# Twelve attention units whose values come out as queries by features, with the softmax sum as a 65th column

## The chip, the cores and the metric

One core of a Trainium2 chip runs the whole program in one launch. The metric is the device time of one execution in microseconds (us); lower is better. Engines are named as in the profile: PE (TensorE, matrix products; PEld its weight loads), DVE (VectorE), ACT (ScalarE), POOL (GpSimd), SP (the queue that issues DMAs).

## The reference, cut to what matters

Three stages follow each other: attention over a window of 128 keys with a distance bias, an expert layer with a squared ReLU, and a mixture of eight experts whose gates are balanced by 8 rounds of normalisation. The change touches the first.

```
B, H, S, D = 4, 8, 576, 64
scores = q @ k.T / sqrt(D)
bias   = slopes[h] * -(|i - j|)              # slopes 2^-(8 (h+1) / H)
scores = where(0 <= i - j < 128, scores + bias, -1e9)
attn   = exp(scores - max(scores));  attn /= sum(attn) + 1e-9
x      = (attn @ v), heads side by side      # 2304 tokens x 512 features
x      = square(relu(x @ w_in)) @ w_out      # first expert layer
out    = sum over 8 experts of gate * relu(x @ w1) @ w2
```

## The kernel before

The attention is cut into 32 units of one batch, two heads (a pair `hp`) and one of two parts: the first 384 queries (three tiles `i` = 0, 1, 2 of 128 queries) or the rest (`rest`: tile 3 of 128 queries and the tail, tile 4, in which 64 queries of both heads share the 128 partitions). The first 12 units (`WHOLE_UNITS`, L56) are worked in a form in which one PSUM bank holds the scores of both heads; these are the four first-part units and the four `rest` units of batch 0, and the four first-part units of batch 1.

Three steps make up a unit, and `plan` (L393) writes down their order. "q" (`attention_qk`, L205) transposes keys and queries. "s" (`attention_scores`, L268) multiplies a tile's queries with two blocks of keys (L289 adds the bias by a product with the identity, L295 the scores), takes the row minimum on DVE (L299), the exponential on ACT with its sum `z` (L314), adds 1e-9 and inverts on DVE (L318, L319) and multiplies the weights `s` by it (L321). "t" transposes the weights block by block (`attention_weights`, L324; PE L345, ACT copy L346 into `p`) and forms the values (`attention_values`, L368, through `block`, L348, PE L354). There the stationary operand is `v` with its 64 features, up to 256 queries move, and the two heads fill the two halves of the output's partitions, so that `xo` is features by queries. `xo` is allocated at tile 1 (in `rest` units at the tail) and complete after the last tile; `put_x` (L359) splits it into the two parts `xh` (ACT, L114) and `xl` (DVE, L115), which the first expert layer reads.

Units 0 to 3 come first, two by two, in an order with two tiles of lead; then chunk 0 of the first expert layer (384 tokens, 16 steps `f`) starts with product `h` (L119 to L121, called from `gemm1`, L123). In each step `part` (L670) advances the attention by a share of the steps of units 4 to 11. In the same steps DVE and ACT convert the 64-bit expert weights (`narrow`, L452), two tiles a step. Units 12 to 31 run beside the later chunks in another form and stay as they are.

PSUM has eight banks of 512 columns here: `ps_acc` (4), `ps_mm` (1) and `ps_at` (3). Units 0 to 3 may use all of them (`at_ps`, L165, by a running count), later units only the three of `ps_at`: for transposed keys and queries (`tp`), scores (`sc`), transposed weights (`pt`) and `xo`.

Up to L738 a planner orders the instructions: it goes by the order in which they were written and by its own idea of when each can run, and fixes each engine's queue. PE's queue and the others run in that order.

Of the kernel before, what the change touches and what calls it, by code (L numbers as in the profile page):

```python
# [8 lines left out]
F32 = mybir.dt.float32  # L9
# [14 lines left out]
def raw(ap):  # L24

    return ap.bitcast(F32)
# [3 lines left out]
def attention_moe_moe2(  # L30
# [12 lines left out]
    nc = tc.nc  # L43
    P = 128
    B, H, S, D = q.shape
# [5 lines left out]
    FULL = S // P  # L51
    TAIL = S - FULL * P
    CH = 512

    EARLY = 3 * P
# [24 lines left out]
    def chunk(c):  # L80
        return starts[c], widths[c]

    xh, xl = [], []
# [11 lines left out]
    ident = const.tile([P, P], F32, name="ident")  # L95
# [17 lines left out]
    def split_ps(ps, hi, lo):  # L113
        nc.scalar.activation(hi, ps, AF.Copy)  # L114
        nc.vector.tensor_sub(lo, ps, raw(hi))  # L115
# [19 lines left out]
    SETS = 2  # L135
# [4 lines left out]
    ap = att.enter_context(tc.tile_pool(name="ap", bufs=1, side="right"))  # L140
# [22 lines left out]
    xo_early = [(ps_mm, "mm"), (ps_acc, "acc")]  # L163

    def at_ps(name, t, many=early):  # L165
        pool, tag = many[psn[0] % len(many)] if t["alone"] else (ps_at, "at")
        psn[0] += 1
        return pool.tile([P, 512], F32, name=name, tag=tag)

    qtail, qwhole = [], []  # L170
    for i in range(SETS):

        qtail.append(ap.tile([P, 2, TAIL], F32, name=f"qtail{i}"))
        qwhole.append(ap.tile([P, 7 * P], F32, name=f"qwhole{i}"))
        nc.gpsimd.memset(qwhole[i], 0.0)

    def tails_ready():

        for i in range(SETS):
            nc.gpsimd.memset(qtail[i], 0.0)  # L180
        for hp in range(NPAIR):
            for j in range(2):
                nc.scalar.copy(
                    tbias[j * TAIL : (j + 1) * TAIL, hp, :], raw(bias[0:TAIL, 2 * hp + j, : P + TAIL])
                )
# [69 lines left out]
    def attention_v(n, t):  # L255

        rest = t["rest"]
        vw = t["v"] = ap.tile([P, 3, 2, D], F32, name="v", tag="v", bufs=2)
        b, hp, _ = units[n]
        for j in range(2):  # L260
            src = v[b, 2 * hp + j]
            if rest:
                nc.sync.dma_start(vw[:, :2, j], src[2 * P : FULL * P].rearrange("(t p) d -> p t d", p=P))
                nc.sync.dma_start(vw[:TAIL, 2, j], src[FULL * P :])
            else:
                nc.sync.dma_start(vw[:, :, j], src[:EARLY].rearrange("(t p) d -> p t d", p=P))

    def attention_scores(hp, t, i):  # L268

        tail = i == FULL  # L270

        kb0, qb0 = (2, 3) if t["rest"] else (0, 0)
        nk = min(S, (i + 1) * P) - max(0, i - 1) * P
        k0 = (max(0, i - 1) - kb0) * P
        c0 = 2 * P - nk if i == 0 else 0
        heads = 1 if tail else 2

        if t["whole"]:
            bank = at_ps("sc", t)
            scs = [bank[:, j * nk : (j + 1) * nk] for j in range(heads)]  # L280
        else:
            scs = [at_ps("sc", t) for j in range(heads)]
        s = ap.tile([P, 2, 2 * P], F32, name="s", tag="s", bufs=3)
        m = ap.tile([P, 2], F32, name="m", tag="m", bufs=3)
        z = ap.tile([P, 2], F32, name="z", tag="z", bufs=3)
        if t["whole"]:
            bj = tbias[:, hp, :nk] if tail else bias[:, 2 * hp : 2 * hp + 2, c0 : c0 + nk]
            sv = bank[:, : heads * nk].rearrange("p (j c) -> p j c", j=heads)
            nc.tensor.matmul(  # L289
                bank[:, :nk] if tail else sv, lhsT=ident_r, rhs=bj, start=True, stop=False,  # L290
                skip_group_check=True,
            )
            for j, sc in enumerate(scs):
                q0 = 6 * P if tail else (2 * (i - qb0) + j) * P
                nc.tensor.matmul(  # L295
                    sc, lhsT=t["qw"][:, q0 : q0 + P], rhs=t["kf"][:, k0 : k0 + nk], start=False, stop=j == heads - 1,
                    skip_group_check=True,
                )
            nc.vector.tensor_reduce(out=m[:, :heads], in_=sv, op=ALU.min, axis=AX.X)  # L299
        else:  # L300
            for j, sc in enumerate(scs):
                r = slice(0, P) if tail else slice(j * D, (j + 1) * D)
                lhs = t["qt"].rearrange("p j c -> p (j c)") if tail else t["qf"][r, (i - qb0) * P : (i - qb0 + 1) * P]
                nc.tensor.matmul(sc[:, :nk], lhsT=lhs, rhs=t["kf"][r, k0 : k0 + nk], start=True, stop=True)
        for j, sc in enumerate(scs if not t["whole"] else ()):
            bj = raw(tbias[:, hp, :nk] if tail else bias[:, 2 * hp + j, c0 : c0 + nk])
            nc.vector.tensor_tensor_reduce(
                out=s[:, j, :nk], in0=sc[:, :nk], in1=bj, scale=1.0, scalar=3.0e38,
                op0=ALU.add, op1=ALU.min, accum_out=m[:, j : j + 1],
            )  # L310
        if tail:
            nc.gpsimd.memset(s[:, 0, nk:], 0.0)
        for j in range(heads):
            nc.scalar.activation(  # L314
                s[:, j, :nk], scs[j][:, :nk] if t["whole"] else s[:, j, :nk], AF.Exp, bias=m[:, j : j + 1], scale=-1.0,
                accum_out=z[:, j : j + 1],
            )
        nc.vector.tensor_scalar_add(z[:, :heads], z[:, :heads], 1e-9)  # L318
        nc.vector.reciprocal(z[:, :heads], z[:, :heads])  # L319
        for j in range(heads):  # L320
            nc.vector.tensor_scalar_mul(s[:, j, :nk], s[:, j, :nk], z[:, j : j + 1])  # L321
        t[i] = s

    def attention_weights(t, i):  # L324

        s, tail, blocks = t[i], i == FULL, 2 if i else 1

        if not t["p"]:
            t["p"] = ap.tile([P, 2, 6 * P], F32, name="p", tag="p", bufs=2)
        kb0 = 2 if t["rest"] else 0  # L330
        at = max(0, 2 * (i - kb0) - 1) * P
        pt = at_ps("pt", t)
        if tail:
            for kb in range(2):
                nc.tensor.transpose(pt[:, kb * P : (kb + 1) * P], s[:, 0, kb * P : (kb + 1) * P], ident)
            for kb, rows in ((0, P), (1, TAIL)):
                c = at + kb * P
                nc.scalar.copy(
                    t["p"][:rows, :, c : c + TAIL], pt[:rows, kb * P : (kb + 1) * P].rearrange("p (j c) -> p j c", j=2)
                )  # L340
            return
        pv = pt[:, : 2 * blocks * P].rearrange("p (j c) -> p j c", j=2)
        for j in range(2):
            for kb in range(blocks):
                nc.tensor.transpose(pv[:, j, kb * P : (kb + 1) * P], s[:, j, kb * P : (kb + 1) * P], ident)  # L345
        nc.scalar.copy(t["p"][:, :, at : at + blocks * P], pv)  # L346

    def block(t, kb, dst, a, w, first, last):  # L348

# [6 lines left out]
                start=first, stop=last, skip_group_check=True,  # L356
            )

    def put_x(ps, hp, t0, n):  # L359
        o = 0  # L360
        while o < n:
            c = max(c for c in range(NCH) if starts[c] <= t0 + o)
            at = t0 + o - starts[c]
            w = min(n - o, widths[c] - at)
            split_ps(ps[:, o : o + w], xh[c][:, hp, at : at + w], xl[c][:, hp, at : at + w])
            o += w

    def attention_values(b, hp, t, i):  # L368

        if i == 1:  # L370
            xo = t["xo"] = at_ps("xo", t, [xo_early[hp % 2]])
            block(t, 0, xo[:, : 2 * P], 0, 2 * P, True, False)
        if i == 2:
            xo = t["xo"]
            block(t, 1, xo[:, P : 3 * P], 0, 2 * P, False, False)
            block(t, 2, xo[:, 2 * P : 3 * P], 0, P, False, True)
            put_x(xo, hp, b * S, EARLY)
        if i == FULL:
            xo = at_ps("xo", t)
            block(t, 3, xo[:, : P + TAIL], 0, P + TAIL, True, False)  # L380
            block(t, 2, xo[:, :P], P, P, False, False)
            block(t, 4, xo[:, P : P + TAIL], 0, TAIL, False, True)
            put_x(xo, hp, b * S + EARLY, P + TAIL)
# [301 lines left out]
    for c in range(NCH):  # L685
        c0, n = chunk(c)
# [15 lines left out]
        for f in range(NF1):  # L702
            now[:] = c, f
            a, bw = ahead.pop(0)
# [4 lines left out]
            hp, tag = (ps_mm, "mm") if c < NCH - 1 else (ps_at, "at")  # L709
# [3 lines left out]
            r = rp.tile([P, CH], F32, name="r", tag="r", bufs=2)  # L713
# [10 lines left out]
            if len(pending) > LAG:  # L724
                t = pending.pop(0)
# [558 lines left out]
```

## Time and profile before

| | us |
|---|---|
| median of 3 runs | 2118.92 |
| lowest, highest | 2118.63, 2123.6 |
| profiled execution, whole | 2118.78 |
| its span in the trace | 2117.0 |

All views are of the one profiled execution, and times in them are microseconds from the start of its span. "Busy" adds up the durations of instructions; on PE matrix products overlap, so the distance from one start to the next tells more of what an instruction costs than its duration. A wait is idle time of an engine just before an instruction, put down to what ended it.

### The profile page before, as it was taken

How to read it: one execution, taken by the hardware profiler on the slowest of the kernel's cores; microseconds unless marked ns; L12 is line 12 of the kernel's file. 1: busy time of each engine (PE TensorE's matmuls, PEld its weight loads, DVE VectorE, ACT ScalarE, POOL GpSimd, SP SyncE). 2: the span in 40 equal slices, each digit the busy share in tenths (PEclk: the TensorE clock that was granted, in tenths of full speed). 3: DMA queues.
4: the chain of work that ended last, by engine and by line, in shares of the span. 5: the costliest groups of instructions: out<-in, count | busy, mean ns of one | idle time of the engine just before them, and what ended most of it. 6: DMA issues, size and time to landing. Idle time of an engine off the chain costs nothing.

```text
span 2117.0 us, 31449 instructions
## 1 busy us (share of the span) xinstructions
PE 2052.1 (97%) x11056; PEld 1859.8 (88%) x11056; DVE 1430.3 (68%) x2396; ACT 958.4 (45%) x1902; POOL 1032.7 (49%) x665
## 2 busy tenths in 40 slices
PE   6999999999998899999999999999999999999998
PEld 4877777777897787899998999999999999999998
DVE  7886444432327888877778676777768676777766
ACT  7775444433334444444444534444445534444343
POOL 1112212122437777888887444455456444455452
PEclk9999999999999999999999999999999999999999
DMA  7686756555667877887888977777887878777773
GB/s 213 227 253 209 230 154 178 158 181 171 210 202 265 294 264 282 307 319 288 309 313 296 319 264 260 256 253 254 266 264 260 271 264 259 256 250 258 264 262 125
DMA packets 281981, 525.43 MB, mean 248 GB/s; under 512 B 85840, under 2 KB 130016, under 8 KB 277728
## 3 DMA queue, kind: packets, MB, share of 16 engines
q1 hardware_dynamic: 281824, 523.42, 73.5%
q8 instruction: 89, 1.46, 0.3%
q14 instruction: 68, 0.56, 0.1%
HBM read 379.60 MB, written 143.73 MB: 247 GB/s over the span
## 4 chain that ended last, share of the span: by engine, by line
PE 59%; DVE 9%; ACT 2%; issue 2%; DMA 1%; POOL 1%; SPq 0%; ACTq 0%; DVEq 0%; POOLq 0%
PE y L120 9%; PE y L121 9%; PE y L119 9%; PE g L119 9%; PE g L121 9%; PE g L120 9%; DVE rl L954 1%; DVE o L922 1%; ACT rh L953 1%; DMA d_w<-w2a 1%; DVE o L920 1%; DVE s L644 1%; DVE s L642 1%; PE acc L120 1%; PE acc L121 1%
## 5 line engine op out<-in xcount | busy, mean ns | idle before, releaser
L1104 POOL TENSOR_TENSOR rb<-R,rb 128x768 fp32r<-128x768 f32 x95 | 212.7, 2239 | 334.6 <-ACT rb L1099 306.2
L1135 DVE TENSOR_TENSOR a<-y,a 128x384 f32<-128x384 f32 x434 | 239.7, 553 | 180.1 <-PE y L121 178.2
L1104 POOL TENSOR_TENSOR rt<-R,rt 128x768 fp32r<-128x768 f32 x125 | 238.9, 1924 | 146.1 <-issue 61.7
L111 POOL TENSOR_TENSOR gl<-r,gh 128x512 fp32r<-128x512 f32 (+1 forms) x80 | 97.1, 1214 | 397.7 <-ACT gh L110 379.1
L111 POOL TENSOR_TENSOR w2a<-r,w2a 128x1024 fp32r<-128x1024 f32 x64 | 155.4, 2430 | 67.5 <-ACT w2a L110 67.5
L1099 ACT ACTIVATE rt<-R 128x768 fp32r<-128x768 f32 x128 | 107.7, 841 | 148.7 <-DVE R L1086 90.2
L119 PE MATMUL g<-xt,w1o 128*128 128x384 f32 x512 | 172.7, 337 | 0.8 <-ACT u L827 0.6
L121 PE MATMUL g<-xt,w1o 128*128 128x384 f32 x512 | 172.4, 337 | 0.0
L119 PE MATMUL y<-rt,w2o 128*128 128x384 f32 x512 | 172.2, 336 | 0.1
L120 PE MATMUL g<-xt,w1o 128*128 128x384 f32 x512 | 172.2, 336 | 0.0
L121 PE MATMUL y<-rt,w2o 128*128 128x384 f32 x512 | 172.2, 336 | 0.0
L120 PE MATMUL y<-rt,w2o 128*128 128x384 f32 x512 | 172.0, 336 | 0.0
L120 PE MATMUL y<-w2a,rh 128*128 128x512 f32 x384 | 151.0, 393 | 0.2 <-POOL w2a L111 0.2
L119 PE MATMUL y<-w2a,rh 128*128 128x512 f32 x384 | 151.1, 393 | 0.0
L121 PE MATMUL y<-w2a,rl 128*128 128x512 f32 x384 | 150.1, 391 | 0.0
L1081 DVE TENSOR_TENSOR R<-R,pb 128x768 f32<-128x768 f32 x128 | 137.8, 1078 | 5.2 <-ACT R L1194 2.4
L716 DVE SCALAR_TENSOR_TENSOR r<-h,r 128x512 f32<-128x512 f32 (+1 forms) x80 | 50.9, 636 | 128.8 <-ACT r L714 128.7
L119 PE MATMUL y<-rb,w2o 128*128 128x384 f32 x384 | 129.8, 338 | 2.8 <-DVE a L1135 2.1
L120 PE MATMUL y<-rb,w2o 128*128 128x384 f32 x384 | 130.0, 339 | 2.4 <-POOL rb L1104 2.4
L121 PE MATMUL y<-rb,w2o 128*128 128x384 f32 x384 | 129.8, 338 | 0.0
L121 PE MATMUL g<-xb,w1o 128*128 128x384 f32 x384 | 129.1, 336 | 0.0
L119 PE MATMUL g<-xb,w1o 128*128 128x384 f32 x384 | 129.0, 336 | 0.0
(232 smaller groups left out, 5892.1 us busy)
## 6 DMA issues: line engine op xcount, KB each, us to landing
w1o<-d_w SPq DMA_DIRECT2D x448, 256.0 KB, 3.1
w2o<-d_w SPq DMA_DIRECT2D x224, 512.0 KB, 4.0
d_w<-w1a SPq DMA_DIRECT2D x32, 1792.0 KB, 11.6
d_w<-w2a SPq DMA_DIRECT2D x32, 1536.0 KB, 7.9
a<-d_in SPq DMA_DIRECT2D x64, 512.0 KB, 3.6
b<-d_out SPq DMA_DIRECT2D x64, 512.0 KB, 3.6
r<-in_moe_w_dram SPq DMA_DIRECT2D x64, 512.0 KB, 4.3
u<-in_moe_w_in_dram SPq DMA_DIRECT2D x16, 512.0 KB, 5.1
```

Of the source, the lines that this page charges most:

```text
L111: (eng or nc.gpsimd).tensor_sub(lo, src, raw(hi))
L119: nc.tensor.matmul(ps, lhsT=lh, rhs=rh, start=first, stop=False, **kw)
L120: nc.tensor.matmul(ps, lhsT=lh, rhs=rl, start=False, stop=False, **kw)
L121: nc.tensor.matmul(ps, lhsT=ll, rhs=rh, start=False, stop=last, **kw)
L642: nc.vector.tensor_sub(w1s[n][:, 2], w1s[n][:, 1], a11)
L644: nc.vector.tensor_sub(w1s[n][:, 0], a12, w1s[n][:, 2])
L716: nc.vector.scalar_tensor_tensor(g[:, :n], ph[:, :n], 0.0, r[:, :n], op0=ALU.max, op1=ALU.mult)
L920: nc.vector.tensor_add(acc[e][:, i], y, acc[e][:, i])
L1081: nc.vector.tensor_mul(r, r, pb[:, None, :].to_broadcast([P, 2, HALF]))
L1099: nc.scalar.activation(x[:, 0], R[m, f, h], AF.Copy)
L1104: eng.tensor_sub(x[:, 1], R[m, f, h], raw(x[:, 0]))
L1135: nc.vector.tensor_add(acc[dst][:, dt], ps[:, :HALF], acc[dst][:, dt])
```

## The change

For the 12 whole units the weights `s` are transposed as they come out of the exponential, without the multiplication by the inverse sum. In the value product the operands change places: a block of transposed weights `p` is stationary (128 keys by 128 queries) and `v` moves, with a 65th column of ones, so that a bank `xq` (128 queries by 65 columns per tile and head) holds the values and the sum of the weights. `vones` are two fixed buffers for `v` whose 65th column is set once. After a unit's last tile one addition, one reciprocal and one multiplication with a broadcast normalise all its tiles, and two or three transposes bring the result to features by queries in a bank `xt`, from which `put_x` goes on; in a `rest` unit it is called three times instead of once. `xq` is allocated at the unit's first tile. The exponential no longer writes its sum.

```diff
+        vones.append(ap.tile([P, 3, 2, D + 1], F32, name=f"vones{i}"))
+        nc.gpsimd.memset(vones[i][:, :, :, D:], 1.0)
...
     def attention_v(n, t):
-        vw = t["v"] = ap.tile([P, 3, 2, D], F32, name="v", tag="v", bufs=2)
+        if t["whole"]:
+            t["v"] = vones[n % SETS]
+            vw = t["v"][:, :, :, :D]
+        else:
+            vw = t["v"] = ap.tile([P, 3, 2, D], F32, name="v", tag="v", bufs=2)
...
     def attention_scores(hp, t, i):
-                accum_out=z[:, j : j + 1],
+                accum_out=None if t["whole"] else z[:, j : j + 1],
             )
+        t[i] = s
+        if t["whole"]:
+            return
         nc.vector.tensor_scalar_add(z[:, :heads], z[:, :heads], 1e-9)
...
     def attention_weights(t, i):
-        if not t["p"]:
+        if t["whole"]:
+            t["p"] = ap.tile([P, 4 * P], F32, name="pw", tag="pw", bufs=3)
+        elif not t["p"]:
...
-        nc.scalar.copy(t["p"][:, :, at : at + blocks * P], pv)
+        if t["whole"]:
+            nc.scalar.copy(t["p"][:, : 2 * blocks * P], pt[:, : 2 * blocks * P])
+        else:
+            nc.scalar.copy(t["p"][:, :, at : at + blocks * P], pv)
...
+    def values_by_query(b, hp, t, i):
+        rest, tail, blocks, W = t["rest"], i == FULL, 2 if i else 1, D + 1
+        u, slots = i - (3 if rest else 0), 2 if rest else 3
+        if u == 0:
+            t["xq"] = at_ps("xq", t, [xo_early[hp % 2]])
+        xq = t["xq"]
+        kb0 = max(0, i - 1) - (2 if rest else 0)
+        for j in range(2):
+            for x in range(blocks):
+                rows = TAIL if tail and x else P
+                at = x * P if tail else (j * blocks + x) * P
+                nc.tensor.matmul(
+                    xq[:, (2 * u + j) * W : (2 * u + j + 1) * W], lhsT=t["p"][:rows, at : at + P],
+                    rhs=t["v"][:rows, kb0 + x, j], start=u == 0 and j == 0 and x == 0, stop=x == blocks - 1,
+                    skip_group_check=True,
+                )
+        if u < slots - 1:
+            return
+        xv = xq[:, : 2 * slots * W].rearrange("p (a d) -> p a d", d=W)
+        z = ap.tile([P, 6], F32, name="zq", tag="zq", bufs=2)[:, : 2 * slots]
+        nc.vector.tensor_scalar_add(z, xv[:, :, D], 1e-9)
+        nc.vector.reciprocal(z, z)
+        y = ap.tile([P, 3, P], F32, name="yq", tag="yq", bufs=2)
+        nc.vector.tensor_mul(
+            y[:, :slots].rearrange("p u (j d) -> p (u j) d", j=2), xv[:, :, :D],
+            z.unsqueeze(2).to_broadcast([P, 2 * slots, D]),
+        )
+        xt = at_ps("xt", t)
+        for x in range(slots):
+            nc.tensor.transpose(xt[:, x * P : (x + 1) * P], y[:, x], ident)
+        if not rest:
+            put_x(xt, hp, b * S, EARLY)
+        else:
+            put_x(xt, hp, b * S + EARLY, P)
+            for j in range(2):
+                put_x(xt[:, P + j * TAIL :], hp, b * S + FULL * P, TAIL, slice(j * D, (j + 1) * D))
...
     def attention_values(b, hp, t, i):
+        if t["whole"]:
+            values_by_query(b, hp, t, i)
+            return
         if i == 1:
-            xo = t["xo"] = at_ps("xo", t, [xo_early[hp % 2]])
+            xo = t["xo"] = at_ps("xo", t)
```

## Rows read from the trace of the kernel before

**Rows 1.** The page, busy time, share of the span and instructions of PE

```profile
PE 2052.1 (97%) x11056; PEld 1859.8 (88%) x11056; DVE 1430.3 (68%) x2396; ACT 958.4 (45%) x1902; POOL 1032.7 (49%) x665
```

**Rows 2.** Busy time by stage: stretch, length, each engine, clock, DMA share, GB/s

```profile
25.40:53.80 28.40, 25.38 (x149) 17.67 (x149) 24.83 (x79) 22.93 (x71) 0.15 (x1) 0.89 0.65 192
53.80:115.00 61.20, 60.15 (x352) 51.92 (x351) 54.38 (x127) 44.73 (x117) 10.82 (x12) 1.00 0.70 224
115.00:180.00 65.00, 58.42 (x327) 45.62 (x326) 58.40 (x143) 47.18 (x121) 7.87 (x8) 1.00 0.78 248
...
216.00:2100.00 1884.00, 1853.21 (x9954) 1702.76 (x9953) 1253.83 (x1946) 807.57 (x1508) 993.31 (x604) 1.00 0.74 252
```

**Rows 3.** Timeline, 22 to 26 us: start, length, instruction, idle before it

```profile
22.82 0.36 ACT L314 ACTIVATE s<-sc,m 128x128 f32<-128x128 f32 x1
25.40 0.45 PE L345 MATMUL pt<-ident,s 128*128 128x128 f32 x1 [7.04 <-DVE s L321]
```

**Rows 4.** PE's waits, 0 to 53.8 (first row), 53.8 to 180: total, times, longest

```profile
PE pt L345 <- DVE s L321: 8.9, 5, 7.0
...
PE sc L289 <- ACT s L314: 1.2, 1, 1.2
PE xo L354 <- ACT s L314: 1.0, 1, 1.0
PE pt L345 <- DVE s L321: 0.9, 3, 0.4
PE tp_k L227 <- ACT p L346: 0.5, 1, 0.5
```

**Rows 5.** Groups by line and shape, DVE, 0 to 180: busy us, mean ns

```profile
L321 DVE TENSOR_SCALAR s<-s,z 128x256 f32<-128x256 f32 x42 | 13.7, 358 | 0.2
L321 DVE TENSOR_SCALAR s<-s,z 128x128 f32<-128x128 f32 x16 | 5.5, 372 | 0.1
L115 DVE TENSOR_TENSOR xl<-xo,xh 128x384 fp32r<-128x384 f32 x4 | 2.2, 548 | 0.0
```

**Rows 6.** Timeline of PE before and as `h` starts

```profile
32.08 0.65 PE L354 MATMUL xo<-p,v 128*64 128x256 f32 x4
32.66 0.50 PE L289 MATMUL sc<-bias,ident_r 128*128 128x512 f32 x1
...
36.23 0.61 PE L295 MATMUL sc<-kf,qwhole 128*128 128x128 f32 x4
36.67 0.60 PE L345 MATMUL pt<-ident,s 128*128 128x128 f32 x4
37.02 0.36 PE L289 MATMUL sc<-bias,ident_r 128*128 128x256 f32 x1
...
53.03 0.87 PE L354 MATMUL xo<-p,v 128*64 128x256 f32 x8
53.84 0.45 PE L119 MATMUL h<-xh,a 128*128 128x384 f32 x1
54.12 0.34 PE L120 MATMUL h<-xl,a 128*128 128x384 f32 x1
54.30 0.33 PE L121 MATMUL h<-xh,a 128*128 128x384 f32 x1
```

**Rows 7.** Timeline of PE, unit 8, one head of block 0

```profile
123.64 0.65 PE L354 MATMUL xo<-p,v 128*64 128x256 f32 x2
124.22 0.38 PE L289 MATMUL sc<-bias,ident_r 128*128 128x256 f32 x1
```

**Rows 8.** Timeline of PE, values of two `rest` units

```profile
66.96 1.03 PE L354 MATMUL xo<-p,v 128*64 128x192 f32 x12
67.92 0.64 PE L227 MATMUL tp<-ident,kraw 128*128 128x128 f32 x3
...
111.05 1.01 PE L354 MATMUL xo<-p,v 128*64 128x192 f32 x8
111.99 0.44 PE L345 MATMUL pt<-ident,s 128*128 128x128 f32 x2
```

More of the change, by code (lines that the diff above doesn't have):

```diff
@@ L168, in at_ps @@
         return pool.tile([P, 512], F32, name=name, tag=tag)
-    qtail, qwhole = [], []
+    qtail, qwhole, vones = [], [], []
     for i in range(SETS):
@@ L321, in attention_scores @@
             nc.vector.tensor_scalar_mul(s[:, j, :nk], s[:, j, :nk], z[:, j : j + 1])
-        t[i] = s
     def attention_weights(t, i):
         s, tail, blocks = t[i], i == FULL, 2 if i else 1
-        if not t["p"]:
+        if t["whole"]:
+            t["p"] = ap.tile([P, 4 * P], F32, name="pw", tag="pw", bufs=3)
+        elif not t["p"]:
             t["p"] = ap.tile([P, 2, 6 * P], F32, name="p", tag="p", bufs=2)
@@ L336, in attention_weights @@
             for kb, rows in ((0, P), (1, TAIL)):
+                if t["whole"]:
+                    nc.scalar.copy(t["p"][:rows, kb * P : (kb + 1) * P], pt[:rows, kb * P : (kb + 1) * P])
+                    continue
                 c = at + kb * P
@@ L357, in block, with put_x @@
             )
-    def put_x(ps, hp, t0, n):
+    def put_x(ps, hp, t0, n, r=slice(0, P)):
         o = 0
@@ L364, in put_x @@
             w = min(n - o, widths[c] - at)
-            split_ps(ps[:, o : o + w], xh[c][:, hp, at : at + w], xl[c][:, hp, at : at + w])
+            split_ps(ps[r, o : o + w], xh[c][r, hp, at : at + w], xl[c][r, hp, at : at + w])
             o += w
+    def values_by_query(b, hp, t, i):
[34 more added lines that the diff above has]
+                put_x(xt[:, P + j * TAIL :], hp, b * S + FULL * P, TAIL, slice(j * D, (j + 1) * D))
     def attention_values(b, hp, t, i):
+        if t["whole"]:
+            values_by_query(b, hp, t, i)
+            return
         if i == 1:
-            xo = t["xo"] = at_ps("xo", t, [xo_early[hp % 2]])
+            xo = t["xo"] = at_ps("xo", t)
             block(t, 0, xo[:, : 2 * P], 0, 2 * P, True, False)
```

## The prediction

> **What bounds the kernel now.** I first read the busy shares of the page, then a table of stages. TensorE (PE) is busy for 97% of the span [rows 1], and the table shows where it is not: it has four stages that matter here [rows 2]. From 216 us to the end PE is busy 1853.2 of 1884.0 us. Nothing of that stretch is touched by the change, and it is bound by PE's own work, so whatever the attention costs or saves ahead of it arrives at the end one for one. The twelve units lie ahead of it: units 0 to 3 before the first matrix product `h` starts at 53.84 us, units 4 to 11 inside chunk 0, up to about 180 us.
>
> In 25.4 to 53.8 us PE is busy 25.4 of 28.4, VectorE (DVE) 24.8; in 53.8 to 115 PE 60.2 of 61.2; in 115 to 180 PE 58.4 of 65.0 and DVE 58.4 too [rows 2]. So PE is nearly full and DVE almost as full, and DVE's weight conversions share its queue with the softmax. The question is which of the two the change presses on. It takes work off DVE and puts work on PE.
>
> The waits of PE say what DVE costs today. Up to 53.8 us the first weights transpose waited 7.0 us, in all 8.9 us in five waits, for the normalised `s` of L321; in 53.8 to 180 the same wait adds up to 0.9 us [rows 4]. PE's idle time from 25.4 to 180 us is 3.0 + 1.0 + 6.6 = 10.6 us [rows 2]. That is all that could be given back there if PE's work stayed as it is.
>
> **The change, part by part.**
>
> *Values as queries by features: PE gets more work.* Before, the stationary operand is `v` (64 columns), both heads stand side by side in the array, and a unit takes six multiplications. I read their cost from starts, not from busy time, which overlaps: block 0 took 32.08 to 32.66 = 0.58 us, blocks 1 and 2 took 53.03 to 53.84 = 0.81 [rows 6]. A change of operand shape costs 0.1 us of lead-in: the first product behind such a block took 53.84 to 54.12 = 0.28, the next 0.18 [rows 6]. With two of these an early unit takes 1.59 us. In chunk 0 three of the four later units show block 0 with the heads apart: 0.58 for one head, 123.64 to 124.22, so 1.16 for both [rows 7], then the same 0.81; with three lead-ins 2.27 us. A `rest` unit in one piece took 66.96 to 67.92 = 0.96, about 1.1 with the lead-in (two units are near that); of the other two one piece alone took 0.94, 111.05 to 111.99 [rows 8], and I estimate 2.0 for the unit with its two small pieces. Sum before: 4 x 1.59 + 3 x 2.27 + 1.59 + 2 x 1.1 + 2 x 2.0 = 21.0 us.
>
> After, the stationary operand is a 128 x 128 block of weights and 65 columns move. A three-tile unit has 2 + 4 + 4 = 10 multiplications; an f32 multiplication stands as two records in the trace, so 20 records, and three transposes of `y`. A `rest` unit has 8, so 16 records, and two transposes. No row of before has 65 columns against 128 stationary ones. The nearest has 128 moving: four records in 36.23 to 36.67, 0.11 each [rows 6]. Scaled by the moving columns it would be 0.055, and that is the lower bound; the upper bound is the 0.11 itself with 0.1 us of lead-in per group of matrices (about 1.2 us more over twelve units). I take 0.109 with the lead-ins, because the four weights transposes right behind them, one record each, took 36.67 to 37.02, still 0.09 each although they do less, so the 128 stationary columns and not the moving ones look like the cost. Sum after: 8 x 23 x 0.109 + 4 x 18 x 0.109 + 1.2 = 29.1 us. PE's work grows by **+8.1 us**, half of it before `h` and half in chunk 0. At the lower price the 224 records cost 224 x 0.055 = 12.3 less, so -4.2.
>
> The Trainium skill weighs on that choice: TensorE: Matmul & The Clock Gate, section LDWEIGHTS (loading the stationary operand), has the load take the columns of the stationary operand divided by 1.2, in ns, whatever the contraction; for 128 columns that is 107 ns, an estimate from that page, and it speaks against this change, which doubles the stationary columns. The rows agree as far as they go (0.11 and 0.09), and by it the sum stays at +8.1.
>
> *The normalisation: DVE loses work, the first wait goes.* The per-tile multiplications of `s` were busy 13.7 and 5.5 us [rows 5], and an addition and a reciprocal on `z` per tile go too; in their place comes one addition, one reciprocal and one 128x384 multiplication per unit, which I bound by the 128x384 subtraction from PSUM, 0.55 us [rows 5]. Busy time overlaps in short instructions; some 10 us of DVE queue come free over twelve units, and ScalarE drops one accumulator read per exponential. What of it is on the path: the first transpose no longer waits for L321. The second of its two exponentials starts at 22.82 and lasts 0.36 [rows 3], so it can start at 23.2 instead of 25.40: **-2.2 us** (bounds 0, if the planner moves those exponentials back, and -2.3). The other waits on L321 are 8.9 - 7.0 + 0.9 = 2.8 us [rows 4]; some turn into waits for the exponential, so **-2.0** (bounds -2.8 and 0). What is late next there is PE itself.
>
> *The end of each unit gets longer.* The last product is now followed by addition, reciprocal, multiplication and transposes before `put_x`; on DVE these stand behind conversions, and the `xt` transposes, and behind them everything on PE's in-order queue, wait for them. For most units other PE work can be placed between; at unit 3 the first `h` needs all four head pairs, but its first three quarters don't need the last pair. I take **+0.5 us** (bounds 0 and 1.5: 0.55 for the multiplication, two short steps, three transposes).
>
> *PSUM buffers.* `xq` now holds a buffer from the first tile of a unit; `xo` was taken at the second (in `rest` units at the last). In chunk 0 there are three such buffers, so the unit's scores, weights and transposed keys turn in two. Waits of PE that look like buffers today: `sc` and `xo` for an exponential, 1.2 and 1.0, and `tp_k` for a copy of `p`, about 0.5 [rows 4], in all 2.7. I expect about 1.5 more, less about 1.0 from the shorter DVE and ScalarE queues: **+0.5** (bounds -2.7 and +8, worked out below).
>
> *At nothing:* the two strided memsets of the ones on GpSimd, whose queue is nearly empty there (0.15 us busy in 28.4 [rows 2]); the `p` copies, equal in size; the two more small `put_x` splits in a `rest` unit, which lie beside the `h` and `acc` products of chunk 0. If that cover failed, they would cost some 0.5 us a unit, an estimate from the 0.55 of the larger subtraction [rows 5].
>
> Sum: +8.1 - 2.2 - 2.0 + 0.5 + 0.5 = +4.9 us. The profiled execution took 2118.78 us (span 2117.0), the median is 2118.92, so the two can be used alike: 2118.8 + 4.9 = **2123.7 us**, +0.23%. A difference under 0.3% (6.4 us) can't be told from none here, so the forecast is no measurable change, on the slow side.
>
> **The rivals.**
> *Slower: the buffer held longer.* Decides from the point at which two buffers turn more slowly than steps come. Some 48 steps in 126 us make one per 2.6 us; a score buffer is released only when its exponentials have run, and `sc` waited 1.2 us for that once [rows 4]. For: idle time is largest in 115 to 180 [rows 2], where the units have three tiles and `xo` is held longest. Against: DVE's queue gets shorter. If each of the eight units of chunk 0 pays one more wait of 0.9 (the mean of the three), that is 7.2 instead of 0.5: 2123.7 + 6.7 = 2130.4.
>
> *DVE was the bound.* Then PE's idle time of 10.6 us is filled by the new work and about half of the added 8.1 us shows, with the 2.2 us at the start gained, so 2118.8 - 2.2 + 4.0 = 2120.6 at most; with all idle time gone 2118.8 - 2.2 + 8.1 - 10.6 = 2114.1, which is the floor, and 2117 lies between. For: DVE at 87 to 90% beside PE [rows 2]. Against: in 53.8 to 115 DVE is just as busy and PE loses 1.0 us in 61.
>
> *The moving columns set the price.* At 0.055 a record the sum is 4.9 - 12.3 = -7.4: 2111.4 us. Against it stands the transposes' row. The same page of the Trainium skill has this rule too, in Back-to-back issue gap: the moving columns over 2.4 plus 2.5 ns, which would be 59 ns for two passes of 65 columns, an estimate; no run here shows it at that width.
>
> *The start is not gained.* The planner orders every queue anew; if conversions stay ahead of the first transposes, the 2.2 us are missing: 2125.9.
>
> **How the numbers follow.** Forecast 0.48 (its own range 2120 to 2128, of which three fifths lie below 2125.2, within 0.3%), buffers 0.22, DVE bound 0.18, moving columns 0.06, start not gained 0.06. Faster by over 0.3%: 0.06 and a little from the DVE case, 0.07. Slower: 0.19 + 0.22 and part of the last, 0.43. The rest, 0.50, within. The range leaves out the moving-column case and the worse half of the buffers: 2116.5 to 2131.
>
> **What would show it.** Records of `xq` about 0.11 us apart (not 0.055); the first L345 transpose near 23 us; `h` starting at 53 to 56 us instead of 53.84; waits of PE for L321 gone; waits of `sc`, `tp_k` or `pt` for a release under 5 us in all in 53 to 180. The prediction is wrong if `h` starts before 51 or after 58 us, or if chunk 0 grows by over 8 us or shrinks.

## The result and the profile after

The changed kernel took 2132.97 us (median of four executions, 2131.46 to 2133.66) against 2119.24 for the kernel before (four, 2118.63 to 2123.6): ratio 1.006, interval 1.0048 to 1.0072, so 13.7 us slower. The forecast was 2123.7, its range ended at 2131: the sign was as forecast, the size almost three times it. The profiled execution took 2133.66 (span 2130.9, against 2117.0 before). Of all executions below one ran slow (7003 us at a granted clock of 0.304, in the kernel with 64 stationary columns) and is left out of its median.

The page's line of busy times of the kernel after, which answers to [rows 1]; per engine busy us, share, instructions:

```profile
PE 2068.5 (97%) x11168; PEld 1884.6 (88%) x11168; DVE 1424.2 (67%) x2316; ACT 954.9 (45%) x1850; POOL 1032.0 (48%) x667
```

PE's share is the same 97%, with 16.4 us more work; DVE has 6.1 us less. Share alone says nothing about the 13.7 us. The table of stages of the kernel after (columns as in [rows 2]), from the start to the first `h` and from there to the first `lt`:

```profile
0.00:61.70 61.70, 41.95 (x213) 33.85 (x214) 35.05 (x76) 35.56 (x80) 9.16 (x30) 0.94 0.64 186
61.70:204.15 142.45, 137.29 (x816) 119.53 (x815) 116.72 (x248) 97.44 (x229) 22.50 (x25) 1.00 0.74 234
```

The same two stretches of the kernel before:

```profile
0.00:53.84 53.84, 34.26 (x182) 23.84 (x182) 41.24 (x118) 38.40 (x107) 9.24 (x29) 0.90 0.72 212
53.84:191.53 137.69, 129.91 (x739) 106.16 (x737) 119.44 (x292) 98.34 (x255) 21.13 (x23) 1.00 0.75 238
```

`lt` is the gate product that ends a chunk's first layer. The first `h` came 7.9 us later and chunk 0 took 4.8 us more. Up to `h` PE has 7.7 us more to do and stands idle as long as before (61.70 - 41.95 = 19.75 against 53.84 - 34.26 = 19.58). In chunk 0 it has 7.4 us more to do and is idle 2.6 us less (5.16 against 7.78). DVE is clearly freer up to the first `h`, 35.05 us busy in 61.70 instead of 41.24 in 53.84, and PE's idle time there is no shorter for it.

To see what the work is, I cut both profiles at the same point of the program, the first `lt` of the fourth chunk (below: the fourth `lt`), and gave each PE record the time to the next record's start, at most its own duration. The sums by tile make up the busy time of that stretch exactly. That stretch in the kernel before, then after:

```profile
0.00:557.11 557.11, 526.27 (x2738) 396.10 (x2738) 304.45 (x870) 285.11 (x742) 113.98 (x126) 0.99 0.64 199
```

```profile
0.00:569.01 569.01, 541.65 (x2850) 420.01 (x2850) 293.53 (x787) 280.18 (x687) 108.99 (x125) 0.99 0.63 193
```

| us up to the fourth `lt` | before | after | difference | forecast |
|---|---|---|---|---|
| value products `xo`, `xq`, with `xt` | 40.5 | 22.5 + 27.6 + 3.3 | +12.9 | +8.1 |
| scores `sc` | 58.1 | 61.6 | +3.5 | 0 |
| `acc` and `h` | 368.6 | 367.5 | -1.1 | 0 |
| other records | 59.1 | 59.2 | +0.1 | 0 |
| PE idle | 30.84 | 27.36 | -3.5 | -3.2 |
| sum | 557.1 | 569.0 | +11.9 | +4.9 |

That is 11.9 of the 13.9 us between the two spans. The last 2.0 lie in the stretch behind it, 1559.9 us before and 1561.9 after; in the profiles of all the kernels below it ran from 1559.6 to 1566.9 us, so nothing is made of them. A record of the value products costs about as much as before (18.0 us of `xo` for 144 records in the twelve units, 0.125 each; 27.6 us of `xq` for 224, 0.123 each); there are 80 more of them, and 32 of `xt`.

PE's waits in the kernel after, first 0 to 70 us, then 53.8 to 200 us (total, times, longest), as in [rows 4]; the two windows overlap:

```profile
PE pt L358 <- ACT s L320: 4.2, 1, 4.2
...
PE xt L414 <- DVE yq L408: 3.1, 4, 1.1
PE xq L396 <- ACT pw L360: 2.7, 5, 0.7
```

```profile
PE xt L414 <- DVE yq L408: 1.2, 2, 0.7
PE xq L396 <- ACT pw L360: 1.0, 2, 0.7
PE acc L119 <- ACT gh L110: 0.7, 1, 0.7
PE sc L295 <- ACT kf L236: 0.6, 1, 0.6
```

The wait of 7.0 us for L321 [rows 4] became one of 4.2 for the exponential. New are the waits for the normalised `yq`, 0.4 to 1.1 us at each of the first four units. For the copied weights PE waits five times, 2.7 us; in the kernel before it did so four times, 1.1 us, in 0 to 70:

```profile
PE xo L354 <- ACT p L346: 1.1, 4, 0.3
```

Timeline of PE after (columns as in [rows 3]): the opening, a group of products, the ends of two units, and the last stretch before `h`:

```profile
22.73 0.73 PE L358 MATMUL pt<-ident,s 128*128 128x128 f32 x2 [4.25 <-ACT s L320]
...
27.93 1.91 PE L301 MATMUL sc<-kf,qwhole 128*128 128x256 f32 x4
29.64 1.06 PE L358 MATMUL pt<-ident,s 128*128 128x128 f32 x4
...
32.88 1.02 PE L301 MATMUL sc<-kf,qwhole 128*128 128x256 f32 x4
33.74 0.33 PE L396 MATMUL xq<-vones,pw 128*128 128x65 f32 x2
...
40.15 1.11 PE L396 MATMUL xq<-vones,pw 128*128 128x65 f32 x8
41.09 1.30 PE L301 MATMUL sc<-kf,qwhole 128*128 128x128 f32 x6
43.26 0.52 PE L414 MATMUL xt<-ident,yq 128*128 128x128 f32 x3 [0.87 <-DVE yq L408]
47.07 0.55 PE L414 MATMUL xt<-ident,yq 128*128 128x128 f32 x3 [1.07 <-DVE yq L408]
...
52.79 1.91 PE L301 MATMUL sc<-kf,qwhole 128*128 128x256 f32 x4
54.49 1.23 PE L396 MATMUL xq<-vones,pw 128*128 128x65 f32 x8
60.54 0.52 PE L414 MATMUL xt<-ident,yq 128*128 128x128 f32 x3 [0.72 <-DVE yq L408]
61.70 0.42 PE L119 MATMUL h<-xh,a 128*128 128x384 f32 x1
```

Two things stand here. Eight `xq` records take 40.15 to 41.09 = 0.94 us, 0.117 each. And four scores of 256 columns take 1.70 us (52.79 to 54.49) where the same four took 0.86 (32.88 to 33.74): there PE ran at half speed. The table of stages around it, kernel after (the column after POOL is the granted clock):

```profile
46.00:50.00 4.00, 2.52 (x14) 2.28 (x15) 1.47 (x4) 1.76 (x5) 0.00 (x0) 0.76 1.03 291
50.00:54.00 4.00, 4.00 (x14) 3.42 (x13) 0.85 (x2) 1.72 (x3) 0.00 (x0) 0.50 0.89 339
54.00:58.00 4.00, 3.71 (x26) 3.21 (x24) 2.58 (x4) 2.11 (x5) 0.00 (x0) 0.88 0.33 85
```

A granted clock of 0.50 is the lower level, 1.2 GHz. Before it fell, PE had been busy only 2.5 of 4 us and had stood still for `yq` twice.

### The profile page after: what moved, and what is told of

Read it like the earlier page. It is cut to its first block, busy times and chain, and to the rows that moved or that the text cites. A ratio compares the mean times of both kernels' runs of the same rounds, so it can differ in the third digit from the quotient of the medians.

```text
span 2130.9 us, 31546 instructions
## 1 busy us (share of the span) xinstructions
PE 2068.5 (97%) x11168; PEld 1884.6 (88%) x11168; DVE 1424.2 (67%) x2316; ACT 954.9 (45%) x1850; POOL 1032.0 (48%) x667
## 4 chain that ended last, share of the span: by engine, by line
PE 57%; DVE 8%; ACT 2%; issue 2%; POOL 2%; DMA 2%; SPq 0%; ACTq 0%; POOLq 0%; DVEq 0%
PE y L120 9%; PE y L121 9%; PE y L119 9%; PE g L119 9%; PE g L121 9%; PE g L120 9%; DVE rl L1011 1%; DMA d_w<-w2a 1%; DVE o L979 1%; ACT rh L1010 1%; DVE o L977 1%; POOL w2a L111 1%; DVE s L701 1%; PE acc L119 1%; PE acc L120 1%
## 6 DMA issues: line engine op xcount, KB each, us to landing
d_w<-w1a SPq DMA_DIRECT2D x32, 1792.0 KB, 11.6
```

## The experiments

The theory at the outset (P): PE's own work sets the time, and the new products cost more, net of the old ones, than I charged. Against it stood the rivals of the prediction: DVE as the bound (D), PSUM buffers, the number of moving columns; later also the half clock and the planner's order. All times are medians beside executions of the kernel before on the same chip; its medians there were 2119.1 to 2119.65, and the kernel after is taken at 2132.97 throughout.

**Early and late units apart.** The new form in units 0 to 3 only, or in 4 to 11 only.

```diff
-        t = {..., "whole": n < WHOLE_UNITS}
+        t = {..., "whole": n < WHOLE_UNITS, "vq": n < NPAIR}      # late: NPAIR <= n < WHOLE_UNITS
...
-        if t["whole"]:       # in attention_v, the scores' end, the weights and the values
+        if t["vq"]:
...
```

> Units 0 to 3 alone take the new form, units 4 to 11 the old one. Theory A, the loss sits in the chain of waits ahead of the first product h: h starts again near 61.7 us (53.84 before), the total is about 8 us over the kernel before. Theory B, the loss is added work of PE, spread over all twelve units: h near 58, the total 4 to 5 us over.

> Units 4 to 11 alone take the new form, units 0 to 3 the old one. Theory A: h starts near 53.8 us and the total is 4 to 6 us over the kernel before (what the changed kernel loses after h). Theory B, added work of PE alone: 8 to 10 us over.

Early alone: 2126.03 against 2119.1, ratio 1.0033 (1.0022 to 1.0044), +6.9 us. Late alone: 2127.78 against 2119.1, 1.0038 (1.0025 to 1.0051), +8.7. Together 15.6, close to the 13.7 of the whole. By the account above, the products with `xt` grew by 5.3 us in the first (`xo` -6.1, `xq` and `xt` +11.4) and by 7.8 in the second (-12.0, +19.8): 13.1 together, 12.9 in the whole. `h` starts at 58.40 and 54.65. The late units came out as the theory of added work said; the early ones have its `h` near 58 but cost more than its 4 to 5 us. So the loss goes with the products wherever they stand, and the start isn't special: the forecast had put about 0 on the early units.

**What sets the price of a record.** Half the moving columns (33, the output is then half of the features, each written twice); half the stationary columns (64, half of the queries are left out; the normalisation then works on 64 partitions of two buffers that are set to zero once).

```diff
-        rest, tail, blocks, W = t["rest"], i == FULL, 2 if i else 1, D + 1
+        rest, tail, blocks, W = t["rest"], i == FULL, 2 if i else 1, D // 2 + 1
...
-                    rhs=t["v"][:rows, kb0 + x, j], ...
+                    rhs=t["v"][:rows, kb0 + x, j, D // 2 :], ...
...
```

```diff
-                    xq[:, ...], lhsT=t["p"][:rows, at : at + P],
+                    xq[:D, ...], lhsT=t["p"][:rows, at : at + D],
...
```

> The changed kernel with 33 instead of 65 moving columns in each value product: half of the features are left out and the other half written twice, all else as it is. Theory S (the 128 stationary columns set the price of a record): records of xq stay 0.11 us apart, the total within 2 us of the changed kernel. Theory M (the moving columns set it): 0.055 to 0.06 apart, the total 10 to 13 us under it.

> The changed kernel with 64 instead of 128 stationary columns in each value product: half of the queries are left out, their values are zero, 65 columns move as they do. Theory S (the stationary columns set the price): records of xq 0.055 to 0.07 us apart instead of 0.114, PE's time in xq falls from 27.6 to 13 to 17 us, the total 8 to 13 us under the changed kernel. Theory M (the moving ones): 0.11 apart, total within 3 us.

Timeline of PE, 33 moving columns: eight records from 39.45 to 40.36, 0.91 us.

```profile
39.45 1.08 PE L396 MATMUL xq<-vones,pw 128*128 128x33 f32 x8
40.36 0.90 PE L301 MATMUL sc<-kf,qwhole 128*128 128x128 f32 x4
```

The same with 64 stationary columns: 38.62 to 39.23, 0.61 us.

```profile
38.62 0.68 PE L401 MATMUL xq<-vones,pw 128*64 128x65 f32 x8
39.23 0.50 PE L300 MATMUL sc<-bias,ident_r 128*128 128x512 f32 x1
```

The median distance between starts inside such a group is 112 ns after, 112 with 33 moving columns and 60 with 64 stationary ones. So at 128 stationary columns it is these that set the price; moving columns change nothing there between 33 and 65. Whether at 64 the 65 moving ones begin to count is not shown. The Trainium skill, TensorE: Matmul & The Clock Gate, section LDWEIGHTS (loading the stationary operand), has the load take the columns over 1.2 in ns: 107 and 53 here, estimates from that page. The trace's 112 agrees; its 60 lies 13% above.

The times: 64 columns took 2129.33 (three executions), 1.0047 (1.003 to 1.0063), 3.6 us less than the kernel after, and `xq` fell by 6.7 us up to the fourth `lt` (27.6 to 20.9), less than 224 x 0.052 = 11.6. The expectation was too high. With 33 columns `xq` stayed at 27.6 us, yet the kernel took 2141.43 (two executions; 1.0102, 1.0083 to 1.012), 8.5 us more than the kernel after. Up to the fourth `lt` PE's work is 5.5 us larger there, spread over `acc`, `h`, `pt` and `sc`. Neither theory said so, and the verdict rests on the distances alone. Most of the 5.5 us can be laid to PE's clock, which was at half in three places (the column after POOL is the granted clock):

```profile
46.00:58.00 12.00, 11.24 (x46) 9.94 (x47) 3.69 (x8) 4.95 (x12) 0.00 (x0) 0.57 0.66 217
61.00:65.00 4.00, 3.84 (x19) 3.65 (x19) 3.60 (x10) 1.66 (x3) 0.00 (x0) 0.57 0.29 65
146.00:150.00 4.00, 4.00 (x19) 3.90 (x19) 3.70 (x7) 1.79 (x3) 0.98 (x1) 0.58 0.04 14
```

By the clock entries of the traces these are 17.0 us at half clock between 35 us and the fourth `lt`, against 6.8 in the kernel after; 10.2 us more at half speed are some 5.1 us of work, an estimate from these lengths. Why the clock fell there more often is open.

**Each product issued twice.** It doubles the new products and leaves the result as it is, since value and sum both double.

```diff
+                for y in range(2):
+                    nc.tensor.matmul(
+                        xq[...], lhsT=..., rhs=..., start=... and y == 0,
+                        stop=x == blocks - 1 and y == 1, skip_group_check=True,
+                    )
```

> The changed kernel with every value product issued twice; the sums double with the values, so the quotient stays. 224 records of xq more, 27.6 us of PE's time in the changed kernel. Theory P (PE's work passes through to the end one for one in both stages): 23 to 28 us over the changed kernel. If PE's idle time covers part of it (theory D, another engine bounds these stages): under 18.

2152.07 against 2119.54, 1.0151 (1.0135 to 1.0166), 19.1 us above the kernel after: between what the two theories asked for. PE up to the fourth `lt`, to be held against the row of the kernel after:

```profile
0.00:584.58 584.58, 562.96 (x3074) 443.27 (x3074) 291.71 (x786) 280.32 (x687) 107.91 (x125) 1.00 0.60 187
```

The products cost 25.9 us more (27.6 to 53.5), other records 4.6 less (`sc` alone 4.0), idle time 5.7 less (27.36 to 21.62): 15.6 us at this mark. Added work passes through at some 60 to 75%; idle time of PE takes up part of it. So the added work doesn't arrive one for one, as theory P had it, and more of it arrives than the under 18 us of theory D.

**DVE relieved in the kernel before.** The normalisation of the whole units is left out (their values are then not normalised).

```diff
-                accum_out=z[:, j : j + 1],
+                accum_out=None if t["whole"] else z[:, j : j + 1],
             )
+        t[i] = s
+        if t["whole"]:
+            return
         nc.vector.tensor_scalar_add(z[:, :heads], z[:, :heads], 1e-9)
```

> The kernel before, leaving out the normalisation of the twelve whole units (accumulated sums, addition, reciprocal, multiplications): its output is not normalised there. PE's work is that of before. It measures alone what the relief of DVE is worth. If the added PE work is the price of the change (theory P: +13 to +15 us of PE work against 3.5 us of idle time given back): 2 to 5 us under the kernel before. If DVE was the bound (theory D): 8 us or more under it.

2124.98 against 2119.65, 1.0024 (1.0015 to 1.0033): 5.3 us slower with less work, which neither theory had. PE's waits in 0 to 200 us:

```profile
PE xo L357 <- DMA v<-in_v_dram: 4.2, 2, 2.7
...
PE sc L289 <- ACT s L314: 2.9, 1, 2.9
```

Neither stands so in [rows 4]: the planner wrote another order, in which PE comes to `xo` before `v` has landed. Idle time as a whole is hardly changed, though (29.7 against 30.8), and `sc` takes 61.4 us instead of 58.1, `xo` 41.8 instead of 40.5. DVE as the bound is hard to hold after this: up to the fourth `lt` DVE lost 20 us (304.45 to 284.39 us busy) and PE's idle time fell by 1.1. Why it is slower by that much is open.

**One instruction less.** Only the addition of 1e-9 to the sums is left out, in all units. The sum holds a term of 1, beside which 1e-9 is lost in float32.

```diff
-        nc.vector.tensor_scalar_add(z[:, :heads], z[:, :heads], 1e-9)
         nc.vector.reciprocal(z[:, :heads], z[:, :heads])
```

> The kernel before without the addition of 1e-9 to the softmax sum: the sum is at least about 1, where the addition changes nothing in f32. One DVE step less between exponential and transposes in every tile. If that chain is what PE waits for (2.8 us after the first wait, and 7.0 us at it): 0.5 to 2 us under the kernel before. If not: no difference within the interval.

2117.05 against 2119.65, 0.9989 (0.998 to 0.9997; eleven executions): 2.6 us faster than the kernel before, the best of all here. The first transposes start 1.1 us earlier than in [rows 3], for a shorter chain on DVE:

```profile
24.31 0.66 PE L344 MATMUL pt<-ident,s 128*128 128x128 f32 x2 [5.99 <-DVE s L320]
```

Idle time of PE up to the fourth `lt` is 25.6 instead of 30.8 us, its work 526.9 instead of 526.3. It keeps the old products, which is the point. Since the order alone moves a time by about as much (below), the shorter chain is the likely cause of the 2.6 us, not a shown one.

**Buffers.** The transposes `xt` go into the bank of `xq` rather than one of their own.

```diff
-        xt = at_ps("xt", t)
+        xt = xq
```

> The changed kernel, but the transposes go back into the bank that held xq, so that a unit takes one PSUM buffer less. If buffers hold back the scores of units 2 and 3 (sc at 50.1 us in the changed kernel), they start 2 us or more earlier, h starts at 57 to 60 us and the total is 2 to 5 us under the changed kernel. If buffers are not the cause: h within 1 us of 61.7, total within 1.5 us, or slower because the next unit's xq waits for the splits.

2132.32 against 2119.1, 1.0059 (1.0044 to 1.0074): the kernel after gave 1.006. `h` starts at 57.11 instead of 61.70, as the buffer theory had it, and PE no longer waits for `yq` ahead of it; but of its 2 to 5 us only 0.7 arrived. A bank less wanted in each unit's end brings nothing that can be told from none, and the longest wait of PE in the kernel after in 53.8 to 200 us is 0.7 (second list of waits above). So buffers are not what costs the 13.7 us.

**The end of a unit and the clock.** Two kernels that both take away most of PE's standing still before `xt` (one wait of 0.7 us is left in the first, none in the second): one turns `xt` a step later in the written order, the other puts five unneeded products ahead of it in units 0 to 3 (40 records).

```diff
+        def finish():
+            xt = at_ps("xt", t)
+            ...
+        late.append(finish)        # run in the next step "t"; at once after units 3 and 11
```

```diff
+        for x in range(5 if t["alone"] else 0):
+            nc.tensor.matmul(
+                xt[:, 3 * P : 4 * P], lhsT=t["p"][:, :P], rhs=ident, start=True, stop=True, skip_group_check=True
+            )
```

> The changed kernel, but the transposes of a unit's normalised values and the splits behind them are issued one weights-and-values step later, so that PE has other work while DVE normalises. Theory A (PE stands still for the normalisation, and its clock falls for it): the waits of xt for yq, 4.3 us in all, go, no stretch at half clock after 45 us, h starts at 55 to 58 us and the total is 4 to 7 us under the changed kernel. Theory B (the work is the price): h stays within 1.5 us of 61.7 and the total within 2 us of the changed kernel.

> The changed kernel with five products whose result is not used ahead of each of the four xt transposes before h, so that PE works while DVE normalises; order and waits of the rest stay near. Theory C (the clock falls in these waits and costs some 3 us): no stretch at half clock after 45 us, the scores at 50 to 55 us at 0.21 us a record instead of 0.43, the total 2 to 4 us under the changed kernel though PE has 40 records more. Without C: the same total or up to 4 us more.

The 4.3 us of the first expectation add up two windows that overlap; the waits for `yq` in the kernel after are 3.1 us.

Stages of the kernel with `xt` a step later, then of the one with the unneeded products:

```profile
46.00:50.00 4.00, 4.00 (x29) 3.56 (x27) 1.38 (x3) 2.09 (x5) 0.00 (x0) 1.00 0.99 373
50.00:54.00 4.00, 3.63 (x30) 3.23 (x29) 2.66 (x8) 3.52 (x8) 0.00 (x0) 1.00 0.68 257
```

```profile
46.00:50.00 4.00, 3.48 (x28) 3.08 (x27) 0.79 (x2) 2.88 (x8) 0.00 (x0) 1.00 0.92 252
50.00:54.00 4.00, 3.71 (x28) 3.26 (x26) 3.43 (x6) 2.58 (x7) 0.00 (x0) 1.00 0.92 352
```

The half clock is gone from this place in both, and a group of four scores of 256 columns has a duration of 1.03 us again (at 46.87 in the one, 49.96 in the other) instead of 1.91. So here the fall goes with the pauses before `xt`. They are not the whole cause, though: the kernel with 64 stationary columns has the same pauses (0.86 and 1.12 us before its first two `xt`), PE is as idle around them, and its clock stays up:

```profile
46.00:50.00 4.00, 2.29 (x21) 1.84 (x22) 1.64 (x5) 2.31 (x8) 0.00 (x0) 1.00 0.74 198
50.00:54.00 4.00, 4.00 (x28) 2.96 (x27) 2.08 (x4) 2.56 (x7) 0.00 (x0) 1.00 1.03 373
```

Nor is the half clock gone for good. It comes later in both kernels, in chunk 0, where the kernel after has none; first `xt` a step later, then the unneeded products:

```profile
100.00:104.00 4.00, 4.00 (x17) 3.76 (x18) 1.49 (x5) 1.35 (x4) 0.00 (x0) 0.57 1.04 397
```

```profile
121.00:125.00 4.00, 4.00 (x15) 3.72 (x15) 1.27 (x4) 0.18 (x1) 0.99 (x1) 0.57 0.90 297
```

The times are 2131.03 (1.005, 1.0035 to 1.0065) and 2131.34 (1.0053, 1.0037 to 1.0068), 1.9 and 1.6 us less than the kernel after, below the 4 to 7 and 2 to 4 us that the theories of the clock had. The second is the cleaner test: the unneeded products cost 4.6 us of PE (`xt` 3.3 to 7.9) and the time still fell. But both gains are no larger than what the order alone moves (below), so what the half clock costs in the end is not shown; it is little beside 13.7 us. In the first, `h` starts at 54.67 instead of 61.70, 7 us earlier, and only 1.9 arrive: what is not done before `h` is done behind it. The start of `h` is no measure of the gain.

**The planner's order.** The running count of PSUM banks starts at 1, in the kernel before and after. No instruction is added or taken away.

```diff
-    psn = [0]
+    psn = [1]
```

> The kernel before with the running count of PSUM buffers of units 0 to 3 started at one: no work added or taken, only which bank each tile gets and with it the planner's order. Theory O (the planner's order alone moves the time by several us): 2 us or more from the kernel before, either way. Otherwise: within 1 us.

> The changed kernel with the same count started at one. Theory O: 2 us or more from the changed kernel's 2133.0, either way. Theory P alone: within 1.5 us of it, since PE's work is the same.

Before: 2119.41 against 2119.54, 0.9996 (0.9986 to 1.0005). After: 2130.73, 1.005 (1.0033 to 1.0067), 2.2 us less than the kernel after. Here order is worth 0 and 2 us, and the change's loss is there in either order (+11.3 between these two). The pair is also the cleanest one for the account, since by the clock entries neither kernel is at half clock between 29 us and the fourth `lt`. That stretch, before and after in the other order:

```profile
0.00:555.50 555.50, 527.60 (x2738) 396.73 (x2738) 307.38 (x870) 285.65 (x742) 114.65 (x126) 1.00 0.63 199
```

```profile
0.00:562.63 562.63, 539.27 (x2849) 416.10 (x2849) 293.52 (x787) 280.54 (x687) 109.31 (x125) 0.99 0.62 195
```

PE's work is 11.7 us larger, the products with `xt` 12.1 (40.6 to 52.7), `sc` 1.7 smaller (61.0 to 59.3), and idle time 4.5 smaller. The `lt` comes 7.1 us later; the rest of the 11.3 arises behind it, where both run the same instructions, and why is open. And `h` starts at 52.93, earlier than in the kernel before:

```profile
52.63 0.55 PE L414 MATMUL xt<-ident,yq 128*128 128x128 f32 x3 [0.36 <-DVE yq L408]
52.93 0.42 PE L119 MATMUL h<-xh,a 128*128 128x384 f32 x1
```

So the late `h`, the long waits for `yq` and the half clock belong to one order of the changed kernel; the larger work of the products belongs to both. The pair also qualifies the 3.5 us on the scores: up to 34 us `sc` takes 9.4 us before and 11.6 after, but 12.8 in the kernel before with the other order, which is not slower. So some 2 us of the 3.5 are the opening, which differs from order to order; four scores at the half clock from 46 to 58 us are 0.84 more.

## Why the prediction was right and wrong

*PE bounds the stretch and work added to it comes through: right in the main, but not one for one.* Halves that add up, doubled products that cost 19.1 us for 25.9 us of work, and a DVE relieved for nothing speak for it.

*The price of an `xq` record: right.* I took 0.109 from the rows with 128 stationary columns [rows 6] against 0.055 from the moving columns; inside a group it is 0.112, and 33 columns cost as much. The rival of the moving columns is out.

*PE's work +8.1: the term that was mis-sized; it is +12.9.* Two errors, both in the same direction. I charged the old form 3.0 us too much (21.0 against the 18.0 that `xo` lost). Some 2.2 of it are its lead-ins; the other 0.7 are the two `rest` units that I estimated at 2.0 and whose products took 1.67 and 1.64 by the account above. The lead-ins I read from the `h` behind a block, 0.28 instead of 0.18 [rows 6], and took them to go away with the block. The new form has such changes of operands too: `acc` and `h` together fell by 1.1 us only, and in the other order they rose by 0.6. And the new form, charged 29.1 with 1.2 of lead-ins, took 30.9 without them, because the first record of a group shows more than the 0.112 (224 `xq` records, 27.6 us, 0.123 each) and some ran at half speed. In the other order, with less of the half clock, the term is still +12.1. It is little in each group and adds up over many.

*Start -2.2 and other L321 waits -2.0: the waits went, the time did not.* The first transpose starts at 22.73 (forecast 23.2), L321 is no longer waited for, but PE's idle time up to `h` is 0.2 us more than before. The waits for `yq` (3.1 us) and longer ones for the copied weights (2.7 instead of 1.1) took much of their place, and the earlier start let PE work where it ran at half speed (last section). The end of a unit, put at +0.5 since "other PE work can be placed between", was the short step here: in this order the planner placed too little ahead of each `xt` in units 0 to 3; in the other order it did, and one wait of 0.4 was left. PE's idle time did fall by 3.5 where the terms net came to 3.2, but in chunk 0 and behind, not at the start. That agreement is luck.

*Not foreseen: the half clock* behind the pauses at the ends of units. The two kernels without these pauses were 1.6 and 1.9 us faster, no more than another order. I had read the clock of the kernel before (0.89 in 25.4 to 53.8 [rows 2]) and not asked what new pauses would do to it.

*Buffers +0.5: no sign of more.* PE's waits for a release stayed under 1 us each, far below the 5 us that would have shown it.

*Signs named in advance.* `xq` records at 0.11, the first transpose near 23, L321's waits gone, few waits for buffers, chunk 0 longer by 4.8 and not over 8: as forecast. `h` at 61.70 instead of 53 to 56: wrong, past the 58 named as refuting it. The sign was a weak one, since the same work in another order has it at 52.93 and is as slow within 2.2 us. It pointed at the early units, where forecast and result differ most (about 0 against +6.9 alone); the late ones were 8.7 against about 5.

*The sum.* It came to 11.9 at the fourth `lt` against 4.9: 4.8 from the products, 3.5 from the scores (opening order and half clock), -1.0 from other records, -0.3 from idle time. With these terms the likeliest case is "slower by over 0.3%" and not "within 0.3%", and the range ended too low above, since it held bounds for the price of a record but none for the cost of the old form and none for PE's clock. In the other order the kernel took 2130.73, just inside it: the work was as mis-sized there.

## What to carry to other kernels

Where PE is the bound, count records and their stationary columns: here 65 or 33 columns moving on 128 stationary ones cost the same, so the swap of operands bought more records at the old price, and relieving another engine didn't buy them back. Lead-ins read in the old form belong to the new one too unless its neighbours change, and a new step at the end of a unit that PE must wait for can cost its wait and PE's clock, depending on the order that the planner finds. Before an effect of 2 us is put down to an edit, run the same edit in another order; two edits here that add no work to PE moved the time by 5.3 and 8.5 us.

## What was not expected of the hardware

In a kernel whose PE is busy for 97% of the span, pauses of about 1 us each, with PE busy 2.5 of 4 us around them, came before a fall of the granted clock to 0.50 (0.76, 0.50 and 0.88 in three stretches of 4 us). Without the pauses the fall was gone from there, but the kernel with 64 stationary columns kept 1.00 with the same pauses, and other kernels fell in chunk 0. So pauses as short as these can come before a fall; what decides it is open.

Earlier in the trace of the kernel after the scores at 27.93 also took 1.71 us for four (27.93 to 29.64), half speed, while the row there reads 1.00. The row of the kernel before for the same time stands below it:

```profile
26.00:30.00 4.00, 3.54 (x11) 2.37 (x10) 1.75 (x4) 2.40 (x6) 0.00 (x0) 1.00 0.35 120
```

```profile
26.00:30.00 4.00, 2.92 (x8) 2.24 (x9) 3.99 (x18) 2.76 (x10) 0.00 (x0) 0.50 0.81 225
```

The two don't contradict each other: the first clock entry in the trace of the kernel after is at 31.05 us, and a row without an entry reads 1.00. The trace of the kernel before has entries from 14.61 us on, and by them PE was at half clock from 21.4 to 31.7. So look where a trace's clock entries begin before reading a row of full clock; distances between starts need no such entry.
